# Attention and a gated MLP on one core: every h by half-size products, running sums kept in PSUM, and new instruction orders

## The chip, the cores and the metric

The kernel runs on one core of a Trainium2 chip. The metric is the device time of one execution in microseconds, as the median of several runs. Of the core's engines, TensorE (PE) multiplies matrices into PSUM (eight banks of 512 float32 per partition), ScalarE (ACT) and VectorE (DVE) work element by element on PSUM and SBUF, GpSimd (POOL) on SBUF, and SyncE (SP) issues most transfers. Each engine works off its own queue in order; semaphores tie the queues together.

## What is computed

Batch 8, 8 heads, 576 positions, head size 64. A linear attention with cosine and sine weights gives x, 4608 tokens of 512; an MLP with 2048 hidden units follows.

```
r(x) = max(x, 0);  q_p = [r(q) cos, r(q) sin],  k_p = [r(k) cos, r(k) sin]     (per position)
kv  = k_p^T v,   z = sum(k_p)
x   = (q_p kv) / (q_p z + 1e-6)              -> (4608, 512)
h   = x @ w_in                               -> (4608, 2048)
g   = h * sigmoid(beta * h)
out = g @ w_out                              -> (4608, 512)
```

## The kernel before

**Tiling.** The 4608 tokens are cut into nine chunks of 512 (0 to 8), the hidden units into 16 tiles of 128 (`jt`). Chunk c of the MLP runs beside the attention of batch c+1, so that PE has work of both kinds. Matmuls are bfloat16 into float32 PSUM. All PSUM is one tile `ps` of eight banks, and the code names banks by number.

**A chunk** has an h part (`xt`, the transposed x of the chunk, times `win`, then a silu on ACT into `g_t`), the attention of its batch (K: k times v into two banks, copied to `kv`; N: the numerators in three parts of two banks each, `num_all`; x: denominator, reciprocal and product on DVE, `x_part` at L319, then a transposing DMA into the next chunks' `xt`), and an output part (`g_t` times `wout`). Around them run the preparation of the next batch's inputs: k relus (ACT, L192), v times sine (ACT, `v`, L218) and cosine (DVE, `w`, L220), q relus (DVE, `q`), the q turn by a transposing DMA (L259), q times the tangent on GpSimd (`g`, L223), and loads of raw q, k and v by SP.

**Half-size products.** Where a 2 by 2 block product would take eight block products, seven are enough, with sums of blocks of the weights (`wh_sums`, `w_sums`, DVE, once), of x (`x_sum`, four per chunk, `t1` to `t4`) and of g (`g_sum`, S1 to S4, L404). For a pair of h tiles each block is 128 rows of weights twice by 256 tokens, so that a pair takes 14 matmuls of 256 columns (L473) in place of eight of 512 (L427). The output goes so in chunks 1 to 8 (`o_fast`, L552, 56 matmuls for each half of the tokens), h in part: four pairs of chunks 3 to 6 (X, Y, Z, V) and six of chunks 7 and 8; the other tiles are plain (`h_plain`, p0 to p7). Chunk 2 takes all h plain (`h_first`).

**A pair's seven products** in `h_fast` use three banks. Bank b gathers 1, 6, 7 and 4, bank e gathers 5 and 3, bank a holds 2. Between them c1 copies b to SBUF (ACT, L498), c5 copies e (DVE, L499), cu copies b again after 6 (ACT, L500), a2 adds c1 to a (DVE, L501), a7 adds c5 to b into b's second half (L502), a3 adds cu to e into a's second half (L503). Then Sa and Sb take the silu of banks a and b (L418). `o_fast` does the same with all three copies on ACT (L598 to L600), adds into the output tile `o_sb` (L602 to L604) and a last copy c4 (L572).

**Order.** The order within chunks 3 to 8 is written out by hand in three strings, `ORDER` (chunks 3 to 6), `ORDER_END` (7) and `ORDER_LAST` (8); `chunk` (its dispatch) records the instructions in this order, engine by engine, and `manual_schedule` keeps it. Loads of the next raw tiles go out when the last reader of the present one is recorded. The q turn (N) waits for the last silu, GpSimd's q product for the first c5 (`after`). `SPLITS` cuts some matmuls of chunks 2 to 5 in two. Stores are issued by GpSimd up to chunk 6, then by SP, and in chunk 8 by SP and ACT.

Of the kernel before, what the change touches and what calls it, by code (L numbers as in the profile page):

```python
# [22 lines left out]
def kernel(  # L23
# [349 lines left out]
    def h_bank(c, jt):  # L373
        if c < 2 and jt < 4:
            return ((3, 2, 5, 0), (6, 7, 4, 5))[c][jt]
        return ((6, 7, 4, 5) if c == 0 else (0, 1, 4, 5))[jt % 4]
# [38 lines left out]
    def h_silu(c, jt, bank):  # L415
        if (c, jt // 4) not in gs:
            gs[c, jt // 4] = gt_pool.tile([P, 4, TCH], BF16, name="g_t", tag="g_t")
        return nc.scalar.activation(gs[c, jt // 4][:, jt % 4], ps[:, bank], AF.Silu, scale=beta[:, jt : jt + 1])  # L418

    def h_plain(c, jt, bank, cols=1):  # L420
        xt = xt_tile(c)
        w = NB // cols
        for mi in range(MI):
            jp, g = divmod(mi, 2)
            for o in range(0, NB, w) if mi else (0,):
                z = o + w if mi else NB
                nc.tensor.matmul(ps[:, bank, o * 64 : z * 64], lhsT=win[jt // 4][:, mi, (jt % 4) * P : (jt % 4 + 1) * P],  # L427
                                 rhs=xt[:, o:z, jp, g * HP : (g + 1) * HP],
                                 start=(mi == 0), stop=(mi == MI - 1 and z == NB))

    def wx_tiles():
# [6 lines left out]
            BF16)[:, 0 : 4 * NB // 2 * P].rearrange("q (s n c) -> q s n c", s=4, n=NB // 2)  # L438
# [6 lines left out]
    def wh_sums(jt):  # L445
        f0 = jt % 4
        A11, A12, A21, A22 = (win[jt // 4][:, 2 * jp : 2 * jp + 2, f * P : (f + 1) * P]
                              for f in (f0, f0 + 1) for jp in range(2))
        s1, s2, s3, s4 = (w_sum(jt, i) for i in range(4))
        nc.vector.tensor_tensor(s1, A21, A22, op=ALU.add)  # L450
        nc.vector.tensor_tensor(s3, A11, A21, op=ALU.subtract)
        nc.vector.tensor_tensor(s2, s1, A11, op=ALU.subtract)
        return nc.vector.tensor_tensor(s4, A12, s2, op=ALU.subtract)

    def x_sums(c):
        xt, n = xt_tile(c), NB // 2
        X11, X12, X21, X22 = (xt[:, i * n : (i + 1) * n, jp] for jp in range(2) for i in range(2))
        t1, t2, t3, t4 = (wx["x"][:, i] for i in range(4))
        nc.vector.tensor_tensor(t1, X12, X11, op=ALU.subtract)
        nc.vector.tensor_tensor(t2, X22, t1, op=ALU.subtract)  # L460
        nc.vector.tensor_tensor(t3, X22, X12, op=ALU.subtract)
        nc.vector.tensor_tensor(t4, X21, t2, op=ALU.subtract)

    def h_fast(c, jt0, banks):

        b_bank, e_bank, a_bank = banks
        hf = TCH // 2
        b_ps, e_ps, a_ps = (ps[:, k, 0:hf] for k in banks)
        xt, n = xt_tile(c), NB // 2

        def prod(dst, left, right, start, stop):
            for g in range(2):
                nc.tensor.matmul(dst, lhsT=left[:, g], rhs=right[:, :, g * HP : (g + 1) * HP], start=start and g == 0,  # L473
                                 stop=stop and g == 1, skip_group_check=True)
# [5 lines left out]
        def x(jp, i):  # L480
            return xt[:, i * n : (i + 1) * n, jp]

        s1, s2, s3, s4 = (w_sum(jt0, i) for i in range(4))
        t1, t2, t3, t4 = (wx["x"][:, i] for i in range(4))
        p1 = part.tile([P, HM], FP32, name="p1", tag="p1")
        p5 = part.tile([P, HM], FP32, name="p5", tag="p5")
        u = part.tile([P, HM], FP32, name="u", tag="u")

        acc = dict(op=ALU.add)
        ops = {  # L490
            "1": lambda: prod(b_ps, w(0, 0), x(0, 0), True, False),
            "5": lambda: prod(e_ps, s1, t1, True, False),
            "6": lambda: prod(b_ps, s2, t2, False, False),
            "2": lambda: prod(a_ps, w(0, 1), x(1, 0), True, True),
            "7": lambda: prod(b_ps, s3, t3, False, False),
            "3": lambda: prod(e_ps, s4, x(1, 1), False, True),
            "4": lambda: prod(b_ps, w(1, 1), t4, False, True),
            "c1": lambda: nc.scalar.copy(p1, b_ps),  # L498
            "c5": lambda: nc.vector.tensor_copy(p5, e_ps),  # L499
            "cu": lambda: nc.scalar.copy(u, b_ps),  # L500
            "a2": lambda: nc.vector.tensor_tensor(a_ps, a_ps, p1, **acc),  # L501
            "a7": lambda: nc.vector.tensor_tensor(ps[:, b_bank, hf:TCH], b_ps, p5, **acc),  # L502
            "a3": lambda: nc.vector.tensor_tensor(ps[:, a_bank, hf:TCH], e_ps, u, **acc),  # L503
            "Sa": lambda: h_silu(c, jt0, a_bank),
            "Sb": lambda: h_silu(c, jt0 + 1, b_bank),
        }
# [27 lines left out]
    SPLITS = {2: (0, 11), 3: (5, 0), 4: (0, 8), 5: (3, 0)}  # L534
    made = {}

    def late(c):
        made[c] = made.get(c, 0) + 1
        return made[c] > 14 - SPLITS.get(c, (0, 0))[1]

    def o_fast(c, pr, banks):
# [3 lines left out]
        last = c == NTC - 1 and pr == 1  # L545

        def prod(dst, left, right, start, stop, pieces=False):
            order = (0, 1, 2, 3, 4, 5, 7, 6) if c + 1 >= B else range(JT // 2)
            for i in order:
                w = HM // 2 if i and pieces else HM  # L550
                for m in range(0, HM, w):
                    nc.tensor.matmul(dst[:, m : m + w], lhsT=left(i), rhs=right[:, i, m : m + w],  # L552
                                     start=start and i == 0,
                                     stop=stop and i == order[-1], skip_group_check=True)
# [16 lines left out]
        def c4():  # L571
            nc.scalar.copy(o2[:, 0:HM], b_ps)  # L572
            if last:
                store(c, pr + 2, o2, 0, HM)

        def stored(key, op):
            def do():
                op()
                waits[key[0]].discard(key[1:])
                if not last and not waits[key[0]]:  # L580
                    store(c, pr + (2 if key[0] == "2" else 0), o2 if key[0] == "2" else o1)
                elif last and key == "1a2":
                    store(c, pr, o1, 0, HM, nc.sync)
                elif last and key[1] == "a":
                    store(c, pr + (2 if key[0] == "2" else 0), o2 if key[0] == "2" else o1, HM, DM)
# [5 lines left out]
            "1": lambda: prod(b_ps, g_part(0, 0), B11, True, False, late(c)),  # L591
            "5": lambda: prod(e_ps, s_part(S1), T1, True, False, late(c)),
            "6": lambda: prod(b_ps, s_part(S2), T2, False, False, late(c)),
            "2": lambda: prod(a_ps, g_part(1, 0), B21, True, True, late(c)),
            "7": lambda: prod(b_ps, s_part(S3), T3, False, False, late(c)),
            "3": lambda: prod(e_ps, s_part(S4), B22, False, True, late(c)),
            "4": lambda: prod(b_ps, g_part(1, 1), T4, False, True, late(c)),
# [8 lines left out]


# [265 lines left out]
    def k_piece(b, j):  # L873
        if b >= B:
            return
        k_relu(b, j, j + 1, "act")
        if j == 3 and b + 1 < B:
            load_raw(b + 1, "k")

    ORDER = (  # L880
        "p0 Y1 X1 c1X p1 X5 c5X g0 g1 sp0 X6 X2 K c1Y X3 cuX kt Y6 X7 p2 a2X a3X Y5 sp1 a7X cuY c5Y Y7 Z1 SaX "
        "X4 c1Z p3 Y3 Y2 SbX sp2 a7Y Z2 s01 Y4 Z5 sp3 Z6 s03 a3Y a2Z p4 SbY V1 a2Y c5Z cuZ Z7 s02 a7Z p5 "
        "SaY c1V V6 Z3 s11 sp4 s12 cuV a3Z V2 Z4 s14 sp5 V5 SbZ c5V V7 p6 a2V V3 SaZ a7V a3V s21 sp6 SaV "
        "p7 s04 s13 V4 s22 SbV s23 sp7 s24 s31 s33 N0 k1 s32 ox1 c1o ox5 k3 c5o k2 ox6 s34 x0 k0 "
        "ox3 oy1 cuo c1y x2 o3x ox2 ox7 v8 oy5 x1 c5y o2x oy6 w8 q0 q1 cuy v2 v6 oy3 o7x v3 w1 oy7 w4 w3 "
        "w7 o7y ox4 v5 t3 w5 oy2 v4 c4x o3y v7 t1 w0 oy4 w6 t2 v1 c4y v0 o2y w2 t4")
    ORDER_LAST = (
        "E1 c1E E2 F1 X1 a2E c1X c1F X5 X2 E5 X6 c5X E6 cuX c5E cuE X3 a2X Y1 E3 X7 a3X c1Y a3E SaX a7X "
        "E7 SaE F6 Y5 F5 a7E X4 Y2 c5F Y6 SbX F2 F3 a2Y c5Y a2F cuF E4 Z1 Y3 cuY SbE c1Z a3F Y7 F7 a3Y "
        "SaF a7Y a7F SaY V1 Z6 Z5 V5 c5V Y4 V2 c1V SbY cuZ F4 Z2 V3 c5Z V6 Z3 p4 Z7 a2V cuV SbF sp4 a3V "  # L890
        "p5 SaV a2Z sp5 a3Z SaZ p6 s13 s01 a7Z Z4 V7 p7 a7V V4 sp6 s11 s03 SbZ ox1 s21 s22 SbV sp7 oy1 "
        "s12 s14 s31 ox2 c1o s32 s02 s34 oy2 s04 oy5 s33 c1y o2x s23 ox6 cuo o2y s24 ox5 ox7 c5y c5o o7x "
        "ox3 oy6 cuy o3x ox4 c4x oy7 o7y oy3 oy4 o3y c4y")
    ORDER_END = (
# [127 lines left out]
    for c in range(2, NTC):  # L1022
# [29 lines left out]
        if c == FAST - 1:  # L1052
            x_sums(c + 1)
# [45 lines left out]
```

## Time and profile before

| what | value |
|---|---|
| median of 3 runs | 277.19 us (276.81 to 278.05) |
| span of the profiled execution | 275.5 us |
| granted clock of PE, mean | 0.999 |
| DMA | 54.0 MB, mean 196 GB/s |
| silu on ACT, 128x512 (L418) | 0.697 us each, 96 of them |
| add on DVE into PSUM, 128x256 (L501 to L503) | 0.42 to 0.43 us |
| copy on ACT, 128x256 (L498, L500) | 0.375, 0.384 us |
| x product on DVE, 128x768 (L319) | 0.957 us |
| q product on GpSimd (L223) | 2.38 us |

The profile is of one execution; its span reaches from the first instruction to the last. Times of single instructions overlap within an engine: the next one starts before the last has written out, so that the spacing of two is shorter than the length of one. A line number names the code line that recorded an instruction.

### The profile page before, as it was taken

The numbers are of one execution on the slowest core, as the hardware profiler recorded it, in microseconds if no ns is written. First come the engines' busy times: TensorE is split into PE (matmuls) and PEld (weight loads), VectorE is DVE, ScalarE is ACT, GpSimd is POOL, SyncE is SP. The second block draws the span as 40 slices with busy tenths as digits, with TensorE's granted clock in tenths as the row PEclk, the third lists the DMA queues.
The fourth block names the chain that finished last, engine by engine and source line by source line (L and its number), as shares of the span: only waits on it lengthen the run. The fifth ranks groups of instructions, "written<-read, shape, count | busy, mean of one in ns | idle before, by whom it ended". The sixth has DMA issues, their size and how long they took to land.

```text
span 275.5 us, 9048 instructions
## 1 busy us (share of the span) xinstructions
PE 268.3 (97%) x3749; PEld 199.8 (73%) x3749; DVE 220.7 (80%) x580; ACT 186.2 (68%) x381; POOL 67.5 (24%) x87
## 2 busy tenths in 40 slices
PE   8899999999999999999999999999999999999993
PEld 8554455456875599869866998688668886888683
DVE  5989969599999899599959985899589589558851
ACT  5778677788238657796669756986694289429821
POOL 1444000500087003800390038102810140000000
PEclk9999999999999999999999999999999999999999
DMA  7999999999969999938893798075400740032005
GB/s 241 370 396 384 392 389 303 385 201 379 240 151 299 209 347 261 366 118 122 195 382 148 119 238 293 28 107 107 114 2 12 117 115 2 1 87 68 2 23 130
DMA packets 50745, 54.00 MB, mean 196 GB/s; under 512 B 31232, under 2 KB 31760, under 8 KB 50704
## 3 DMA queue, kind: packets, MB, share of 16 engines
q1 hardware_dynamic: 47744, 45.88, 59.9%
q0 software_dynamic: 2688, 7.34, 8.7%
q8 instruction: 29, 0.48, 0.7%
q10 hardware_dynamic: 272, 0.21, 0.3%
q14 instruction: 12, 0.10, 0.1%
HBM read 36.71 MB, written 9.44 MB: 168 GB/s over the span
## 4 chain that ended last, share of the span: by engine, by line
PE 86%; DMA 9%; DVE 2%; SPq 1%; issue 1%; ACTq 0%; ACT 0%; DVEq 0%
PE ps L552 36%; PE ps L473 16%; PE ps L427 13%; PE ps L384 12%; DMA raw_q<-in_q_dram 6%; PE ps L297 4%; DMA raw_v<-in_v_dram 3%; PE ps L522 3%; PE ps L276 2%; SPq L79 1%; DVE xs L319 1%; PE ps L235 0%; PE ps L356 0%; DVE win L115 0%; DVE vb L210 0%
## 5 line engine op out<-in xcount | busy, mean ns | idle before, releaser
L418 ACT ACTIVATE g_t<-ps,beta 128x512 bf16<-128x512 f32 x96 | 60.9, 697 | 3.2 <-DVE ps L503 2.8
L515 POOL DMA_DIRECT2D out_dram<-o_sb x56 | 33.1, 597 | 118.1 <-DVE o_sb L602 43.4
L552 PEld LDWEIGHTS <-S 128*128 128x128 bf16 x589 | 51.4, 98 | 5.1
L384 PE MATMUL ps<-xt,win 128*128 128x512 bf16 (+1 forms) x196 | 42.8, 375 | 0.1
L552 PEld LDWEIGHTS <-g_t 128*128 128x128 bf16 x440 | 38.2, 98 | 4.1
L427 PE MATMUL ps<-xt,win 128*128 128x512 bf16 (+1 forms) x184 | 40.8, 351 | 0.0
L392 ACT ACTIVATE g_t<-ps,beta 128x512 bf16<-128x512 f32 x48 | 32.3, 689 | 7.2 <-PE ps L384 7.1
L384 PEld LDWEIGHTS <-win 128*128 128x128 bf16 x196 | 18.8, 98 | 21.0 <-issue 0.2
L552 PE MATMUL ps<-wout,g_t 128*128 128x256 bf16 (+1 forms) x284 | 31.7, 262 | 0.0
L552 PE MATMUL ps<-wout,S 128*128 128x256 bf16 (+1 forms) x305 | 31.5, 255 | 0.0
L552 PE MATMUL ps<-T,S 128*128 128x256 bf16 (+1 forms) x284 | 30.8, 262 | 0.0
L404 DVE TENSOR_TENSOR S<-g_t 128x512 bf16<-128x512 bf16 (+1 forms) x66 | 26.1, 423 | 3.6 <-ACT g_t L418 2.7
L218 ACT ACTIVATE vb<-raw_v,sin 128x256 bf16<-128x256 f32 (+1 forms) x58 | 25.9, 501 | 2.2 <-DMA raw_v<-in_v_dram 2.2
L473 PEld LDWEIGHTS <-w_stage 128*128 128x128 bf16 x224 | 21.6, 98 | 6.7
L473 PE MATMUL ps<-w_stage 128*128 128x256 bf16 x168 | 26.2, 272 | 0.0
L427 PEld LDWEIGHTS <-win 128*128 128x128 bf16 x184 | 17.9, 98 | 10.1
L319 DVE TENSOR_TENSOR xs<-ps,rden 128x768 bf16<-128x768 f32 (+4 forms) x26 | 22.8, 884 | 0.8
L220 DVE TENSOR_SCALAR vb<-raw_v,cos 128x256 bf16<-128x256 f32 x63 | 20.0, 374 | 0.8 <-DMA raw_v<-in_v_dram 0.8
L473 PEld LDWEIGHTS <-win 128*128 128x128 bf16 x168 | 16.4, 98 | 4.7 <-issue 0.3
L223 POOL TENSOR_TENSOR qs<-qt,tanr 128x1152 bf16<-128x1152 bf16 x6 | 14.2, 2381 | 21.4 <-DVE den L308 21.0
L473 PE MATMUL ps<-xt,win 128*128 128x256 bf16 x112 | 19.1, 272 | 0.0
L599 ACT COPY p<-ps 128x256 f32<-128x256 f32 x16 | 5.9, 372 | 16.9 <-PE ps L552 13.8
(105 smaller groups left out, 418.3 us busy)
## 6 DMA issues: line engine op xcount, KB each, us to landing
raw_v<-in_v_dram SPq DMA_DIRECT2D x7, 1152.0 KB, 10.8
raw_k<-in_k_dram SPq DMA_DIRECT2D x7, 1152.0 KB, 7.5
raw_q<-in_q_dram SPq DMA_DIRECT2D x7, 1152.0 KB, 7.4
out_dram<-o_sb POOLq DMA_DIRECT2D x56, 128.0 KB, 4.1
w_stage<-in_moe_w_in_dram SPq DMA_DIRECT2D x3, 1024.0 KB, 13.9
w_stage<-in_moe_w_out_dram SPq DMA_DIRECT2D x2, 1024.0 KB, 8.8
w_stage<-in_moe_w_out_dram SPq DMA_DIRECT2D x4, 512.0 KB, 11.9
out_dram<-o_sb SPq DMA_DIRECT2D x12, 128.0 KB, 2.4
```

The lines of the kernel that those rows point to most:

```text
L218: nc.scalar.activation(o, a, AF.Copy, scale=t[:, n : n + 1])
L220: nc.vector.tensor_scalar(o, a, scalar1=t[:, n : n + 1], scalar2=None, op0=ALU.mult)
L223: return eng.tensor_tensor(dst.rearrange("q n (g p) -> q n g p", g=2), src.rearrange("q n (g p) -> q n g p", g=2), tanr[:, n0:n1].unsqueez ...
L319: nc.vector.tensor_tensor(o.rearrange("q j n s d -> q j (n s) d"), nv[:, :, a:z, :, 0:D].rearrange("q j n s d -> q j (n s) d"), rden[:, :, ...
L384: nc.tensor.matmul(ps[:, h_bank(c, jt), i * 64 : (i + w) * 64], lhsT=win[jt // 4][:, mi, (jt % 4) * P : (jt % 4 + 1) * P], rhs=xt[:, i : i ...
L392: return nc.scalar.activation(gs[c, jt // 4][:, jt % 4], ps[:, h_bank(c, jt)], AF.Silu, scale=beta[:, jt : jt + 1])
L404: return nc.vector.tensor_tensor(o, l, r, op=op)
L418: return nc.scalar.activation(gs[c, jt // 4][:, jt % 4], ps[:, bank], AF.Silu, scale=beta[:, jt : jt + 1])
L427: nc.tensor.matmul(ps[:, bank, o * 64 : z * 64], lhsT=win[jt // 4][:, mi, (jt % 4) * P : (jt % 4 + 1) * P], rhs=xt[:, o:z, jp, g * HP : (g ...
L473: nc.tensor.matmul(dst, lhsT=left[:, g], rhs=right[:, :, g * HP : (g + 1) * HP], start=start and g == 0, stop=stop and g == 1, skip_group_ ...
L515: (eng or own).dma_start(out=out_v[bb, n][:, m0:m1], in_=o_sb[hf * HP : (hf + 1) * HP, m0:m1])
L552: nc.tensor.matmul(dst[:, m : m + w], lhsT=left(i), rhs=right[:, i, m : m + w], start=start and i == 0, stop=stop and i == order[-1], skip ...
```

## The change

All eight pairs of h go by half-size products in chunks 3 to 8, by `h_pair`; the output of chunks 2 to 8 by `o_pair`. Chunk 1 keeps `o_fast`; chunk 2 keeps its plain h, with two tiles in other banks. Both new functions share `fast_ops`, which uses two banks for a pair. Bank b's halves hold the running sum (1, 6, 7, 4) and product 5. c (the seed) copies the running sum into the first half of bank a, where product 2 adds; d or D copies product 5 to SBUF on ACT or DVE; e adds that copy to the running sum after 6, into the second half of bank a, where 3 adds; f does the same after 7, into the second half of b (for the output, into `o_sb`). A and B take the silu of a whole bank (for the output, A or X copies bank a, 512 wide, on ACT or DVE, B or Y the first half of b).

The order is now one string for each of chunks 2 to 8, and names the bank of every product 1, seed, K and N. Tokens: `h35` is product 5 of pair 3, `h3c7` its seed into bank 7, `oxe` the e of the output's first token half, `s13` S1 of tiles 6 and 7, `W71` sum 1 of the weights of pair 7, `TQ` the q turn of the next batch, `Lv` a load; x, k, v, w, q, g and t as above. The t sums of two chunks lie in two places (`4 * (c % 2)`), so that they can be made while the last ones are read. The weight sums of pairs 1, 3, 5 and 7 are made in chunk 3. The q turn and GpSimd's q products wait for their data alone, the kv copy is on ACT (`kT`), and `SPLITS` is gone.

```diff
@@ h_bank, h_silu, wx_tiles
+        if c == 2 and jt in (10, 11):
+            return jt - 8
-        return nc.scalar.activation(gs[c, jt // 4][:, jt % 4], ps[:, bank], AF.Silu, scale=beta[:, jt : jt + 1])
+        return nc.scalar.activation(gs[c, jt // 4][:, jt % 4], bank, AF.Silu, scale=beta[:, jt : jt + 1])
-            BF16)[:, 0 : 4 * NB // 2 * P].rearrange("q (s n c) -> q s n c", s=4, n=NB // 2)
+            BF16).rearrange("q (s n c) -> q s n c", s=8, n=NB // 2)
...
+    def sum_tile():
+        tag = ("p5", "p1", "u")[len(sums) % 3]
+        sums.append(part.tile([P, HM], FP32, name=tag, tag=tag))
+        return sums[-1]
+
+    def fast_ops(left, right, prod, finish):
+        st = {}
+        def bank(key):
+            return ps[:, st[key]]
+        def at(key, hf):
+            return bank(key)[:, hf * HM : (hf + 1) * HM]
+        def first(n):
+            st["b"] = n
+            prod(at("b", 0), left(0), right(0), True)
+        def seed(n):
+            st["a"] = n
+            nc.scalar.copy(at("a", 0), at("b", 0))
+        def keep(eng):
+            st["p5"] = sum_tile()
+            (nc.scalar.copy if eng == "act" else nc.vector.tensor_copy)(st["p5"], at("b", 1))
+        def add(dst):
+            nc.vector.tensor_tensor(dst, at("b", 0), st["p5"], op=ALU.add)
+        return {
+            "1": first,
+            "5": lambda: prod(at("b", 1), left(1), right(1), False),
+            "c": seed,
+            "d": lambda: keep("act"),
+            "D": lambda: keep("dve"),
+            "6": lambda: prod(at("b", 0), left(2), right(2), False),
+            "2": lambda: prod(at("a", 0), left(3), right(3), False),
+            "e": lambda: add(at("a", 1)),
+            "7": lambda: prod(at("b", 0), left(4), right(4), False),
+            "3": lambda: prod(at("a", 1), left(5), right(5), False),
+            "f": lambda: finish(add),
+            "4": lambda: prod(at("b", 0), left(6), right(6), False),
+        }, bank, at
+
+    def h_pair(c, i):
...
+        ops, bank, at = fast_ops(lefts.__getitem__, rights.__getitem__, prod, lambda add: add(at("b", 1)))
+        ops["A"] = lambda: h_silu(c, jt0, bank("a"))
+        ops["B"] = lambda: h_silu(c, jt0 + 1, bank("b"))
...
+    def o_pair(c, pr):
...
+        def finish(add):
+            add(sb_tile("2")[:, HM:DM])
+            stored(1)
+        def take(key, eng):
+            copy = nc.scalar.copy if eng == "act" else nc.vector.tensor_copy
+            if key == "a":
+                copy(sb_tile("1"), bank("a"))
+                store(c, pr, sb["1"])
+            else:
+                copy(sb["2"][:, 0:HM], at("b", 0))
+                stored(0)
...
+        4: (
+            "g1 h114 h15 h015 h05 h211 K02 h1d h0d h0c7 K1 h1c0 h06 h0e h16 h25 kT h12 h312 h02 h2D h03 h2c6 h07 h1e "
+            "h17 h13 h0A h3c7 h0f h26 h1f h413 h1A h04 g0 h2e h45 h4c0 h0B h35 h4D h36 h23 h14 h27 h3d h22 h2f h46 h1B "
+            "h3e h515 h55 h24 h2A h2B h37 h32 h33 h5D h714 h4e h75 h616 h3f h43 h5c1 h34 h3A h6c7 h47 h56 h7d s10 h42 "
+            "h66 h3B h4f h65 h44 h7c2 h6d h62 s20 h5e h76 h52 h57 h4B h53 h6e h7e h5f h63 h73 h72 h4A h77 h5A h67 s11 "
+            "TQ N00 w5 h7A w7 h6f h7f h54 h6A s21 oy13 h74 h64 v6 ox12 v8 x0 N10 h5B s30 s12 h6B s33 h7B oyc7 w1 N25 "
+            "s13 s22 v4 oy5 x1 v5 s23 s42 ox5 oxc4 oxd k2 s32 oy2 oy6 k1 s31 oyd v3 w2 w4 s41 ox6 s40 oye t1 ox2 oy7 "
+            "v7 k3 q0 oxe q1 s43 oyf k0 ox7 w3 t2 v2 w0 oxf oy3 oy4 x2 w8 ox3 oyA v0 w6 oyB v1 Lv Lk oxA ox4 t3 t4 oxY"),
...
-    FAST = 3
+    h_first(2)
     for c in range(2, NTC):
...
+        chunk(c)
```

The last tokens of chunk 8 are `oxY oy3 oy2 oyY oyA`.

## The prediction

> **What bounds the kernel now.** First the page's busy shares and the chain that ended last:
>
> ```profile
> PE 268.3 (97%) x3749; PEld 199.8 (73%) x3749; DVE 220.7 (80%) x580; ACT 186.2 (68%) x381; POOL 67.5 (24%) x87
> PE 86%; DMA 9%; DVE 2%; SPq 1%; issue 1%; ACTq 0%; ACT 0%; DVEq 0%
> ```
>
> TensorE (PE) is busy for 97% of the span and makes up 86% of the chain. The chain's 9% of DMA lies before 40 us, in code that the change leaves alone. Next the chain in order of time, for the unit prices (start, length, what, how many matmuls):
>
> ```profile
> 139.93 1.15 PE ps L276 x72
> ...
> 151.38 1.38 PE ps L297 x130
> ...
> 180.91 12.33 PE ps L552 x112
> ...
> 221.23 6.78 PE ps L473 x62
> 228.01 0.86 PE ps L427 x4
> ```
>
> A 512-column matmul of a plain h costs 0.864/4 = 0.216 us; a 256-column matmul of a half-size product costs 6.78/62 = 0.1093. K (k times v) costs 1.15, the numerators N 1.38. Then busy time chunk by chunk (chunk 2 after its h, chunks 3 to 8, the tail):
>
> ```profile
> core 0: us, PE busy (x) PEld busy (x) DVE busy (x) ACT busy (x) POOL busy (x), PEclk, DMA share, GB/s
> 95.09:109.09 14.00, 14.00 (x334) 13.41 (x335) 12.24 (x35) 8.99 (x21) 2.28 (x5) 1.00 1.13 290
> 109.09:137.11 28.02, 28.02 (x433) 23.26 (x431) 23.41 (x66) 20.63 (x44) 9.17 (x10) 1.00 0.75 204
> 137.11:165.24 28.13, 28.13 (x474) 22.59 (x472) 23.41 (x65) 21.03 (x45) 9.30 (x11) 1.00 0.81 225
> 165.24:193.25 28.01, 28.01 (x426) 22.69 (x425) 23.76 (x70) 21.05 (x45) 8.92 (x10) 1.00 0.55 132
> 193.25:221.23 27.98, 27.98 (x418) 21.84 (x417) 20.76 (x56) 15.68 (x33) 8.95 (x11) 1.00 0.31 60
> 221.23:246.15 24.92, 24.92 (x214) 20.73 (x213) 18.10 (x51) 15.95 (x36) 2.06 (x4) 1.00 0.19 46
> 246.15:270.40 24.25, 24.25 (x206) 19.96 (x205) 16.58 (x45) 15.91 (x36) 0.00 (x0) 1.00 0.22 50
> 270.40:275.50 5.10, 0.86 (x8) 0.52 (x6) 0.42 (x1) 0.37 (x1) 0.00 (x0) 0.97 0.48 118
> ```
>
> The reader is to see that PE has no gap from chunk 2 on, at full clock. So what PE no longer does is gained, as long as ScalarE (ACT) and VectorE (DVE) keep up. Their pace comes from the timeline of chunk 4:
>
> ```profile
> 143.72 2.43 ACT L418 ACTIVATE g_t<-ps,beta 128x512 bf16<-128x512 f32 x4
> ...
> 147.06 0.36 ACT L498 COPY p<-ps 128x256 f32<-128x256 f32 x1
> 147.32 0.70 ACT L418 ACTIVATE g_t<-ps,beta 128x512 bf16<-128x512 f32 x1
> ...
> 147.43 0.42 DVE L404 TENSOR_TENSOR S<-g_t 128x512 bf16<-128x512 bf16 x1
> 147.88 0.42 DVE L404 TENSOR_TENSOR S<-S,g_t 128x512 bf16<-128x512 bf16 x1
> ```
>
> Four silus (0.69 each) take 2.43, so one follows another after (2.43-0.69)/3 = 0.58; a copy holds ACT for 0.26 to 0.27. Where an instruction needs its own engine's previous result (S2 needs S1) it starts at 0.45 instead of at 0.33, the spacing of independent ones: 0.03 after the end.
>
> **What PE loses.** A pair of h by half-size products takes 14 x 0.1093 = 1.53, plain 8 x 0.216 = 1.73. After the change a chunk 3 to 6 is 112 x 0.1093 = 12.24 of h, 12.24 of output, K and N: 27.01. Four of them are 108.04 against 112.14: -4.10. Chunk 7 falls to 24.48 from 24.92: -0.44. Chunk 8 really ends at 270.40+0.86, so it falls from 25.11 to 24.48: -0.63. Chunk 2's output loses the matmuls cut into 128 columns (SPLITS): 12.24 + 1.36 of N against 14.00: -0.40. Sum with no stall: -5.57. It includes the 0.1 us or so of gaps and split costs that each chunk has now.
>
> **What ACT and DVE get.** Per pair, three copies and three adds become a seed (ACT, PSUM to PSUM), one copy and two adds. But all eight pairs have them now. ACT work per pair is two silus 1.16 + seed 0.27 + 5/8 of a copy 0.17 = 1.60, against 1.53 of PE. So in the h part ACT becomes as slow as PE, where today half of the pairs are plain and ask for silus alone. Seeds have a second price: in the changed program's waits, five of a steady chunk's eight seeds write a bank that the silu just ahead of them on ACT is still reading, so they wait for ACT's own end: 0.69+0.03 instead of 0.58, some 0.14 each. No row shows this wait on ACT; from below it is 0, from above 0.14 by the DVE row, which I take.
>
> Chunk 4 walked to the place where it binds: the first silu needs the 12th product of PE's order, with K ahead of it, 12 x 0.2186 + 1.15 = 3.77, and ACT starts 0.21 later (silus in chunk 2 start 0.21 after the last matmul's turn ends): 3.98. Before pair 7's seed ACT has 8 silus 4.64, six copies 1.62 and five such waits 0.70: the seed starts at 10.94, is done at 11.31 (0.37), and PE may go on 0.05 later (a copy of kv ended at 11.97, the matmul behind it began at 12.02): 11.36. PE wants it for product 6 of pair 7 after 44 products, at 44 x 0.2186 + 1.15 = 10.77. Stall 0.59; with no own-wait cost, none. Behind it on PE stands the rest of the chunk. Orders 5 and 6 are the same up to bank numbers. For the three I take 0.55 each: 1.65.
>
> Chunk 3 has four seeds of this kind and sixteen weight sums more on DVE (W; eight of them came in chunk 5 so far, eight are new) at 0.20 spacing: 3.2. DVE's queue in chunk 3 is then 25.6 (W 3.2, S 5.3, adds and copies of h 6.3, x 4.0, output 1.7, w 2.35, q 1.36, t 1.33; by their spacing in the timeline: 0.33 for an S, an add or a t, 0.26 a w, 0.68 a q, 1.33 an x with its reciprocal) of 27.0. Behind a late W stands product 5 of a pair, behind a late S the output's product 5. I take 0.8, between 0 and 1.6. Chunks 7 and 8 have no K and no v, but also less PE work between their silus: 0.4 each. Given back in all: 1.65+0.8+0.8 = 3.25, with bounds 0.5 and 6.5.
>
> **Edits at no cost.** The kv copy moves from DVE to ACT (0.59), in the 1.15 of K in which ACT has little to do; uncovered, it delays the first silu by as much. The q turn (a transposing DMA on SP's queue, which today waits behind the silus) goes out at a chunk's start, past nothing on SP but the loads, and lands before N some 13 us later. GpSimd's two q products (2.38 each) no longer wait for a copy; N comes late enough to hide both and the stores queued around them. The v load is used earlier: ACT takes v5 at some 13.6 us into chunk 3, today its first v at 20. The load went out at 109.32 and such loads took up to 11.9, so it lands at 121.2, 12.1 into the chunk. Cover 1.5; if it is gone, each us is a us of PE, since the last silus stand behind v5 on ACT.
>
> **Tail.** The last product is now followed by a 512-column ACT copy (0.60 by L528) and 128 KB stores (2.4 to landing) in place of a 256-column copy (0.37) and 64 KB (2.0 to 2.2): +0.5, bounds 0.2 and 0.8.
>
> **A rule against the change.** PSUM halves that used to sit in three banks share one now, and the changed program guards by bank: a seed waits for product 5 too (0.22), product 6 for both copies (0.27). Today product 5 has a bank of its own. The Trainium skill, page "PSUM — Partial Sum Buffer", section "PSUM bank collisions raise a hardware error", asks for just that: guard by bank, not by address. By it every pair's chain is 0.22+0.27 longer; by the walk above this is hidden behind other pairs' products, so the sum would differ only if eight banks were too few. The page "ScalarE: Activation LUTs" ("Step-by-step: what each stage is for") speaks the other way: ACT writes PSUM faster than SBUF. No run here shows it yet; it would shorten the 0.37.
>
> **Sum.** -5.57 + 3.25 + 0.5 = -1.8 on the span of 275.5: 273.7. The median of the runs lies 1.7 above that span (277.19): 275.4.
>
> **Rivals.** (1) ACT is not the limit: own-engine waits cost nothing and DVE's load spreads. For it: the walk then has no stall at all. Against: ACT has 1.60 of work per 1.53. -5.57+0.3+0.5: 272.4. (2) Given back nearly whole: stalls of 0.8 to 1 in every chunk, since an output stage whose DVE work (13 S, x, w, q, t and its adds, by the same prices some 15 us, in 13.7 of PE) sits behind late silus adds its own. -5.57+5.3+0.5: 277.4. (3) Slower, by one mechanism: the seed. No row shows ACT writing PSUM; if it takes 0.1 longer than a copy to SBUF (by the rows of the copies 0, by DVE's adds, 0.42 into PSUM against 0.42 into SBUF, 0 too), eight seeds in six ACT-bound chunks add 4.8: 280.2. It decides from 0.067 each: 1.8+1.4 = 3.2 over 48 seeds. That the products are not really replaced is excluded by the program's matmul count.
>
> **How the numbers follow.** 0.5% (1.4 us) is about what a measurement of this kernel can tell from no change: 275.8 and 278.6 are the limits. Forecast, 273.9 to 276.4: 0.46, of which 0.33 below 275.8. Rival 1: 0.25. Rival 2: 0.17. Rival 3: 0.12. Faster 0.33+0.25 = 0.58, same 0.13+0.17 = 0.30, slower 0.12. The range 272.6 to 277.8 leaves out rival 3 and the ends of 1 and 2.
>
> **What would show it.** Right: chunks 4 to 6 some 27.6 long, with PE idle of about 0.5 each just ahead of products 6 of the later pairs, put down to ACT; ACT without a gap between first silu and last; chunk 3 longest; PE's sum 5 us smaller. Wrong: chunks of 27.0 (rival 1), gaps in the output part put down to DVE (rival 2), seeds over 0.45 (rival 3), or ACT waiting for a v load.

## The result, and the profile after it

| | before | after |
|---|---|---|
| median, us (four runs each) | 277.16 (276.81 to 278.05) | 284.25 (283.40 to 284.38) |
| span of the profiled execution, us | 275.5 | 281.6 |
| mean granted clock of PE | 0.999 | 0.988 |

The changed kernel takes 1.0243 times as long (95% interval 1.0223 to 1.0264): slower, and outside the predicted range. First the page of the changed kernel: busy time, PE and its clock in forty slices (tenths), the chain that ended last.

```profile
PE 268.9 (95%) x3712; PEld 208.0 (74%) x3712; DVE 225.6 (80%) x588; ACT 192.7 (68%) x391; POOL 67.0 (24%) x87
PE   8899999999999999399999999999999999999993
PEclk9999999999999999689999999999999999999999
PE 82%; ACT 6%; DMA 3%; issue 3%; DVE 3%; SPq 1%; DVEq 0%
```

The shares differ little from before. The rows by slices say where to look: in the seventeenth PE has a 3, and the clock has 6 and 8 in place of 9 in this one and the next. A slice is 7 us. Now busy time chunk by chunk (chunks 3 to 8, each from the end of the last matmul before it):

```profile
core 0: us, PE busy (x) PEld busy (x) DVE busy (x) ACT busy (x) POOL busy (x), PEclk, DMA share, GB/s
108.58:143.80 35.22, 30.30 (x443) 25.10 (x441) 31.65 (x83) 23.86 (x52) 9.21 (x11) 0.90 0.54 148
143.80:171.76 27.96, 27.68 (x442) 24.08 (x441) 23.43 (x65) 22.98 (x51) 9.64 (x12) 1.00 0.65 192
171.76:199.73 27.97, 27.70 (x443) 24.05 (x441) 22.39 (x64) 22.95 (x50) 8.92 (x11) 1.00 0.72 167
199.73:227.71 27.98, 27.70 (x442) 24.07 (x441) 19.89 (x53) 17.31 (x37) 8.93 (x11) 1.00 0.30 61
227.71:252.31 24.60, 24.60 (x226) 21.86 (x225) 17.69 (x48) 15.03 (x32) 2.48 (x5) 1.00 0.22 59
252.31:277.41 25.10, 24.82 (x225) 21.67 (x222) 15.96 (x43) 15.39 (x34) 0.00 (x0) 1.00 0.24 56
```

Chunk 3 takes 35.22 where it took 28.02 before: +7.20, more than the whole loss. The chunks 4 to 6 are 0.21 shorter together (84.12 to 83.91), chunk 7 is 0.32 shorter, chunk 8 with the tail 0.06. The rest of the span's difference is a start of chunk 2's output that lies 0.39 earlier (94.70 in place of 95.09) and 0.12 less in that output (13.88 in place of 14.00): 7.20-0.21-0.32-0.06-0.39-0.12 = 6.1. So the question is chunk 3 alone. Two windows of it (columns as above), and the instructions around them (start, length, engine, line, tiles, in brackets the idle time before it and what ended it):

```profile
111.84:117.09 5.25, 0.39 (x4) 0.20 (x3) 5.25 (x3) 0.15 (x1) 4.70 (x2) 0.83 1.04 397
117.09:122.14 5.05, 5.04 (x24) 3.49 (x24) 2.86 (x11) 3.08 (x6) 0.00 (x0) 0.50 0.91 174
```

```profile
110.93 0.29 DVE L443 TENSOR_TENSOR w_stage<-win 128x256 bf16<-128x256 bf16 x1
111.13 5.57 DVE L443 TENSOR_TENSOR w_stage<-win,w_stage 128x256 bf16<-128x256 bf16 x1
116.62 0.42 DVE L487 TENSOR_TENSOR ps<-ps,u 128x256 f32<-128x256 f32 x1
...
111.83 4.71 POOL L223 TENSOR_TENSOR w_stage<-qt,tanr 128x1152 bf16<-128x1152 bf16 x2
...
111.63 0.60 PE L511 MATMUL ps<-xt,win 128*128 128x256 bf16 x4
117.09 0.58 PE L511 MATMUL ps<-xt,win 128*128 128x256 bf16 x2 [4.86 <-DVE ps L487]
```

Read from below. PE waits 4.86 for an add on DVE (L487). The add stands in DVE's queue behind one sum of weight blocks (L443), and that sum takes 5.57 where its like take 0.28 to 0.29. It ends at 116.70, when GpSimd's two q products end (111.83+4.71 = 116.54). The idle time has a second price: from 117.09 the granted clock is 0.50 for 5.05, in which 24 matmuls run that take 24 x 0.1093 = 2.62 at full clock, so 2.43 more. 4.86+2.43 = 7.29, which is all of the 7.20.

In the kernel before, the same two products ran at nearly the same time, and the sign was there:

```profile
76.69 4.73 POOL L223 TENSOR_TENSOR qs<-qt,tanr 128x1152 bf16<-128x1152 bf16 x2 [20.98 <-DVE den L308]
79.53 4.14 DVE L220 TENSOR_SCALAR vb<-raw_v,cos 128x256 bf16<-128x256 f32 x9
...
109.89 0.29 DVE L453 TENSOR_TENSOR w_stage<-win,w_stage 128x256 bf16<-128x256 bf16 x1
112.04 4.72 POOL L223 TENSOR_TENSOR w_stage<-qt,tanr 128x1152 bf16<-128x1152 bf16 x2 [0.95 <-DVE p L499]
113.12 0.70 DVE L288 CAST kv<-ps 128x520 bf16<-128x520 f32 x1 [1.17 <-PE ps L276]
116.44 0.94 DVE L404 TENSOR_TENSOR S<-g_t 128x512 bf16<-128x512 bf16 x2 [0.52 <-ACT g_t L418]
```

In chunk 3 the weight sums of that kernel were over before GpSimd began behind a copy of DVE, and until 116.44 DVE had copies and adds that read PSUM: nothing was held. The first S sum at 116.44 took 0.60 in place of 0.42 and ended at 117.04, behind GpSimd's end at 116.76. At 79.53, beside another pair of products, nine v products took 4.14 where nine at their spacing of 0.26 take about 2.4: the first alone took 2.04 in place of 0.35 and ended at 81.57, just after GpSimd at 81.42.

### The profile page after: what moved, and what is told of

The parts are those of the page before. It is cut to its first block, busy times and chain, and to the rows that moved or that the text cites. A ratio compares the mean times of both kernels' runs of the same rounds, so it can differ in the third digit from the quotient of the medians.

```text
span 281.6 us, 8955 instructions
## 1 busy us (share of the span) xinstructions
PE 268.9 (95%) x3712; PEld 208.0 (74%) x3712; DVE 225.6 (80%) x588; ACT 192.7 (68%) x391; POOL 67.0 (24%) x87
## 4 chain that ended last, share of the span: by engine, by line
PE 82%; ACT 6%; DMA 3%; issue 3%; DVE 3%; SPq 1%; DVEq 0%
PE ps L620 31%; PE ps L511 21%; PE ps L386 14%; PE ps L543 5%; ACT g_t L420 4%; PE ps L562 4%; PE ps L297 4%; DMA raw_v<-in_v_dram 3%; PE ps L276 3%; ACT ps L480 1%; DVE ps L487 1%; DVE xs L319 1%; SPq L79 1%; PE ps L356 0%; DVE win L115 0%
## 5 line engine op out<-in xcount | busy, mean ns | idle before, releaser
L511 PE MATMUL ps<-w_stage 128*128 128x256 bf16 x288 | 48.2, 277 | 0.9 <-ACT ps L480 0.7
L511 PEld LDWEIGHTS <-w_stage 128*128 128x128 bf16 x384 | 38.0, 100 | 7.9 <-issue 2.1
L487 DVE TENSOR_TENSOR ps<-ps,p 128x256 f32<-128x256 f32 x74 | 30.5, 428 | 16.4 <-PE ps L511 7.8
L386 PE MATMUL ps<-xt,win 128*128 128x512 bf16 (+1 forms) x196 | 42.8, 375 | 0.1
L511 PE MATMUL ps<-xt,win 128*128 128x256 bf16 x192 | 35.3, 278 | 5.1 <-DVE ps L487 4.9
L480 ACT COPY ps<-ps 128x256 f32<-128x256 f32 x62 | 22.4, 370 | 12.7 <-PE ps L620 8.6
L620 PE MATMUL ps<-wout,g_t 128*128 128x256 bf16 x224 | 28.8, 273 | 0.0
L620 PE MATMUL ps<-T,S 128*128 128x256 bf16 x224 | 27.0, 273 | 0.0
L620 PE MATMUL ps<-wout,S 128*128 128x256 bf16 x224 | 26.7, 273 | 0.0
L487 DVE TENSOR_TENSOR ps<-ps,u 128x256 f32<-128x256 f32 x36 | 15.4, 428 | 6.8 <-PE ps L511 4.8
```

The lines of the kernel that those rows point to most:

```text
L386: nc.tensor.matmul(ps[:, h_bank(c, jt), i * 64 : (i + w) * 64], lhsT=win[jt // 4][:, mi, (jt % 4) * P : (jt % 4 + 1) * P], rhs=xt[:, i : i ...
L480: nc.scalar.copy(at("a", 0), at("b", 0))
L487: nc.vector.tensor_tensor(dst, at("b", 0), st["p5"], op=ALU.add)
L511: nc.tensor.matmul(dst, lhsT=l[:, g], rhs=r[:, :, g * HP : (g + 1) * HP], start=start and g == 0, stop=g == 1, skip_group_check=True)
L620: nc.tensor.matmul(dst, lhsT=l(i), rhs=r[:, i], start=start and i == 0, stop=i == order[-1], skip_group_check=True)
```

## The experiments

**What made chunk 3 long.** Theory A: a DVE instruction that takes two tiles from SBUF is held while a GpSimd product runs. The test takes GpSimd's products of batch 4 out of chunk 3 and puts them behind the last S sum of chunk 2, where DVE has x products, reading PSUM, to do. The rival, B: the q turn, now at a chunk's start, is what delays it.

```diff
         2: (
-            "oy16 N22 x2 N00 oy5 ...
+            "oy16 G0 G1 N22 x2 N00 oy5 ...
         3: (
-            ... h1A h23 W52 g0 "
+            ... h1A h23 W52 "
...
-            ... h72 s11 g1 h7A ...
+            ... h72 s11 h7A ...
+            elif k_ == "G":
+                q_tan(b + 1, n, None if n else last_sum)
...
```

> Edit: GpSimd's two q products of batch 4 (2.38 us each) are recorded at the start of chunk 2's output part, behind chunk 2's last S sum on DVE, instead of in chunk 3; all else as in the changed kernel. Theory A (GpSimd's products and DVE's sums of two SBUF operands shut each other out: the weight sum at 111.13 that took 5.57 us ended 0.2 us after GpSimd's pair of products): no weight sum over 0.3 us in chunk 3, PE's 4.9 us gap gone, no half clock behind it, chunk 3 28 to 29 us instead of 35.4, total 284.3 - 6.5 to 7.5 = 277 to 278. Theory B (the q turn, which now goes out at the start of chunk 3 and took 9.8 us, slows DVE's SBUF accesses): the long sum stays, total 283 to 285. Theory C (the sixteen weight sums of chunk 3 are simply too much for DVE): chunk 3 stays over 31, total over 280.

Measured: 276.6 us (276.1 to 278.48), ratio to before 0.9978 [0.9955, 1.0000], a little under the 277 to 278 of theory A. Three lines of its timeline:

```profile
97.69 4.74 POOL L223 TENSOR_TENSOR w_stage<-qt,tanr 128x1152 bf16<-128x1152 bf16 x2 [10.12 <-DMA qt<-qb]
...
101.29 1.29 DVE L443 TENSOR_TENSOR w_stage<-win 128x256 bf16<-128x256 bf16 x1
...
112.42 0.28 DVE L443 TENSOR_TENSOR w_stage<-win,w_stage 128x256 bf16<-128x256 bf16 x1
```

The weight sum that took 5.57 takes 0.28, and the loss of 7 us is gone with it. Chunk 3 lasts 28.28 from its K to the next one's with all sixteen weight sums in it, so theory C falls. GpSimd issues stores from 108.75 to 113.22, so beside stores alone this sum is not held. In chunk 2 one weight sum still meets the products: started at 101.29, it lasts 1.29, to 102.58, just after GpSimd's end at 102.43. So 7 us hang on which instruction of DVE meets the same work of GpSimd.

The rival's test, the q turn back behind the last silu:

```diff
-                    q_turn_dma(b + 1)
+                    q_turn_dma(b + 1, last)
```

> Edit: the q turn of chunks 3 to 5 waits for the last silu recorded ahead of it, as in the kernel before; GpSimd's products stay where the changed kernel has them. Theory A: the weight sum of some 5.6 us stays at the start of chunk 3, total 283.5 to 285. Theory B: the long sum is gone, total 277 to 279.

Measured: 283.52 (282.89 to 284.13), 1.0212 [1.0173, 1.0251], with the same sum of 5.57 and the same wait of 4.86. B falls.

**Is it the guard, or what DVE does meanwhile?** Two more kernels leave the products in chunk 3 and give them a guard again, one behind weight sum W53, one behind W74, the chunk's last.

```diff
-                wh_sum(2 * n, int(op[2]))
+                parts[op] = wh_sum(2 * n, int(op[2]))
...
-                q_tan(b, n)
+                q_tan(b, n, parts.get("W53"))
```

> The changed kernel, with GpSimd's two products of chunk 3 held back by a guard, as in the kernel before, here behind the weight sum W53. Theory A: they run from about 116.5 to 121.2, and the next DVE instruction with two SBUF inputs, S sum s30 due at 117.5, is held to about 121.2 (some 3.7 us in place of 0.42), the copies and adds behind it with it; PE idles 3 to 3.7 and the time is 279 to 282, the upper end if PE's clock halves again. Rival theory (it was the missing guard as such, or the products' early start, that cost the time): with the guard back, 276 to 277.

> The changed kernel, with GpSimd's two products of chunk 3 behind the chunk's last weight sum W74. Theory A: they run from about 118.1 to 122.9, where DVE has only copies and adds on PSUM until the S sums due at 121.4; these are held 1.4, and N (due at 122.4) waits some 0.5 for the products: 276.0 to 277.5, no sum over 2 us. Rival (any GpSimd product in chunk 3 costs what it cost): over 280.

Measured: 280.69 (278.68 to 281.48), 1.0092 [1.0062, 1.0121], behind W53, and 278.18 (277.34 to 279.44), 1.0027 [1.0007, 1.0047], behind W74, a little over its range. The timeline behind W53:

```profile
116.22 4.90 POOL L223 TENSOR_TENSOR w_stage<-qt,tanr 128x1152 bf16<-128x1152 bf16 x2 [3.95 <-DVE w_stage L443]
...
117.13 0.43 DVE L487 TENSOR_TENSOR ps<-ps,p 128x256 f32<-128x256 f32 x1
117.47 1.41 DVE L406 TENSOR_TENSOR S<-g_t 128x512 bf16<-128x512 bf16 x1
118.81 2.46 DVE L443 TENSOR_TENSOR w_stage<-win,w_stage 128x256 bf16<-128x256 bf16 x1
...
122.10 0.38 PE L511 MATMUL ps<-w_stage 128*128 128x256 bf16 x2 [1.95 <-ACT ps L480]
```

The add on PSUM at 117.13 keeps its 0.43 beside GpSimd; the S sum behind it takes 1.41 and the weight sum 2.46, to GpSimd's end. The S sum got through where GpSimd's first product gives way to its second (116.22+2.4); so the hold was by the product here. The forecast of one sum held for the whole time was wrong in that, and its 3 to 3.7 of idle PE too long (about 2.4, 2.1 of it in one piece); the time lies in its range. Behind W74 two S sums took 2.13 in place of 0.75, and PE waited 0.28 for the products and 0.80 for an add. A guard helps as far as it moves the products beside DVE work that is not held.

The clock has a part in these runs too. In the profiled one, at full clock, PE idles those 2.4 (by the spacing of its matmuls); of ten runs six had a mean clock of 0.990 to 0.994 and took 281.05 on average, four had 0.997 to 1.000 and took 278.92. The drop came with some of the runs only, and these took 2.1 longer; whether PE also idled longer in them isn't shown.

**What the chunks 4 to 6 give back.** With chunk 3 mended, PE's gaps are few: 0.20 and 0.40 ahead of the seeds of pairs 6 and 7 in each of the chunks 4 to 6, 0.40 in chunk 8, none in chunk 7, some 0.6 in chunk 3. That is the forecast stall. (These gaps go by the spacing of the starts; the brackets of the timeline count from the modelled end of the matmul before, and have 0.23 for 0.40.) ACT shows why (chunk 4 of the changed kernel):

```profile
147.71 0.69 ACT L420 ACTIVATE g_t<-ps,beta 128x512 bf16<-128x512 f32 x1
148.43 0.36 ACT L480 COPY ps<-ps 128x256 f32<-128x256 f32 x1
148.70 0.69 ACT L420 ACTIVATE g_t<-ps,beta 128x512 bf16<-128x512 f32 x1
...
155.10 0.38 PE L511 MATMUL ps<-w_stage 128*128 128x256 bf16 x2 [0.23 <-ACT ps L480]
```

A seed behind a silu of its own bank starts 0.72 after that silu's start, not 0.58. To test it, the seeds of pairs 5 to 7 go to DVE (a new token C), once on the changed kernel and once with the early products.

```diff
+        def seed_dve(n):
+            st["a"] = n
+            nc.vector.tensor_copy(at("a", 0), at("b", 0))
...
-            ... h43 h5c1 h34 h3A h6c7 h47 h56 h7d s10 h42 "
-            "h66 h3B h4f h65 h44 h7c2 h6d h62 s20 h5e ...
+            ... h43 h5C1 h34 h3A h6C7 h47 h56 h7d h42 "
+            "h66 h3B h4f h65 h44 h7C2 h6d s10 h62 s20 h5e ...
```

> Edit: in chunks 4 to 6 the seeds of pairs 5, 6 and 7 are copied by DVE instead of ACT, and S1 of tiles 0 and 1 is taken a few places later; chunk 3 as in the changed kernel. Theory D (in chunks 4 to 6 PE waits for ACT, whose seeds start 0.72 us behind the silu that they must wait for, not 0.58): ACT is relieved by 3 x (0.27 + 0.14) = 1.2 us ahead of pair 7's product 6, the 0.84 us that the h part loses per chunk falls to 0.3 or less, chunks 4 to 6 go from 27.97 to 27.2 to 27.5, total 284.3 - 1.5 to 2.3 = 282 to 282.8. Rival E (the loss comes from PSUM banks that come free late, or from DVE): no change within 0.4, or slower, since DVE gets 3 x 0.33 us more.

> Edit: the products early and the DVE seeds together. Theories A and D: the gains add, 284.3 - 7 - 2 = 275 to 276, which is 0.4 to 0.8% below the kernel before. If either falls: 277 or more.

Measured: 284.72 (283.81 to 285.87), 1.0265 [1.0224, 1.0306], and with the early products 277.7 (276.76 to 279.02), 1.0007 [0.9983, 1.0030]: no gain. In the second:

```profile
147.98 0.42 DVE L406 TENSOR_TENSOR S<-g_t 128x512 bf16<-128x512 bf16 x1
148.43 0.43 DVE L406 TENSOR_TENSOR S<-S,g_t 128x512 bf16<-128x512 bf16 x1
148.78 0.42 DVE L491 TENSOR_TENSOR ps<-ps,u 128x256 f32<-128x256 f32 x1
...
149.25 0.38 PE L516 MATMUL ps<-xt,win 128*128 128x256 bf16 x2 [0.62 <-DVE ps L491]
```

ACT's stall is gone, and PE waits 0.62 for an add that now stands behind two S sums. Next, the two sums behind the adds of pair 5; and, on top, the weight sum that was held in chunk 2 moved behind the q relus, and the seed of pair 4 of chunk 8 on DVE.

```diff
-            "h66 h3B h4f h65 h44 h7C2 h6d s10 h62 s20 h5e h76 h52 h57 h4B h53 h6e h7e h5f h63 ...
+            "h66 h3B h4f h65 h44 h7C2 h6d h62 h5e h76 h52 h57 h4B h53 h6e h7e h5f s10 s20 h63 ...
```

> As the run with GpSimd's products in chunk 2 and the seeds of pairs 5 to 7 on DVE, but the two S sums of chunks 4 to 6 that stood before the adds e of pair 5 now stand behind f of pair 5. Theory D (ACT's own-engine waits cost 0.60 of PE a chunk, and with the seeds on DVE the two sums, 0.8 on DVE, cost the 0.78 gap in their place): the gap before product 3 of pair 5 goes and no other comes, chunks 4 to 6 are 27.3 to 27.4 long in place of 27.96, and the time is 276.6 - 1.8 = 274.8. Rival (what is short is the chain of copies and adds itself, wherever the sums stand): a gap of 0.4 to 0.8 stays in each of the chunks 4 to 6, time 276.5 to 277.7.

> As the run before it, with the first sum of the weights of pair 6 moved behind the two q relus in chunk 2 (it was held 1.0 us by GpSimd's products) and with the seed of pair 4 in chunk 8 on DVE (PE waited 0.40 for it on ACT). Theory A (DVE sums of two SBUF tiles are held while GpSimd's product runs, DVE work on PSUM or with one SBUF tile is not): no DVE sum over 0.45 us in chunk 2, PE's gap of 0.55 there is gone, though GpSimd works in the same 4.7 us; with chunk 8 another 0.4: 0.9 less than the run before it, 273.9. Rival (GpSimd slows any DVE work beside it): the gap in chunk 2 stays, 274.4.

Measured: 276.22 (275.41 to 278.38), 0.9956 [0.9933, 0.9978], and 276.25 (276.01 to 278.54), 0.9959 [0.9936, 0.9982]. Misses by 1.4 and 2.3. The gaps of the h part are gone, but chunk 4 lasts 28.09 from its K to the next one's: PE now stalls in the output part, ahead of N for an x product on DVE and once more behind it (0.35 and 0.32). In chunk 8 DVE's seed made two gaps, 0.48 and 0.43, out of one of 0.40. The chunk 2 part held: GpSimd worked from 97.04 to 101.77, no sum of DVE lasted over 0.45, PE had no gap. The sentence on single SBUF tiles, though, has the v products at 79.53 against it, and no run here tests them.

The two moves alone (products and weight sum), all seeds on ACT:

> The changed kernel with GpSimd's products of batch 4 in chunk 2 and the weight sum that they held there moved behind the q relus; all seeds on ACT. Theory A: PE's gap of 0.55 in chunk 2 goes, the 0.60 in each of the chunks 4 to 6 and the 0.40 in chunk 8 stay: 276.6 - 0.5 = 276.1. Rival (the gap in chunk 2 is covered by a later wait anyway): 276.6.

Measured: 276.41 (276.03 to 277.62), 0.9958 [0.9940, 0.9976]; the gap of 0.55 is gone from its trace, but the time, between the two forecasts, can't tell them apart. With earlier seeds on DVE, those of pairs 3 and 4 (`h3c7` to `h3C7`, `h4c0` to `h4C0`, and `h5c6` to `h5C6` in chunk 8):

> As the run with the two moves, and the seeds of pairs 3 and 4 of chunks 4 to 6, and of pair 5 in chunk 8, on DVE: there DVE waits (0.73 and 0.77 in chunk 4, 0.95 in chunk 8) while ACT has no gap. Theory E (ACT and DVE share one sum of work, and work moved costs only where the taker has no idle time before its own queue is full, in chunk 4 from 149 on): PE's gaps of 0.60 go without new ones in the output part, chunks 4 to 6 are 27.4 in place of 27.96, chunk 8 0.4 shorter: 2.1 less than the run with the two moves, 274.0. Rival (whatever ACT is relieved of, DVE gives back later, as with the seeds of pairs 5 to 7): chunks 4 to 6 stay at 27.8 to 28.0, time 275.6 to 276.2.

Measured: 277.54 (277.02 to 279.0), 1.0000 [0.9981, 1.0019]. A miss, and worse than none:

```profile
141.81 0.43 DVE L484 COPY ps<-ps 128x256 f32<-128x256 f32 x1 [0.83 <-ACT g_t L420]
142.15 0.75 DVE L491 TENSOR_TENSOR ps<-ps,p 128x256 f32<-128x256 f32 x2
...
142.62 0.38 PE L516 MATMUL ps<-w_stage,win 128*128 128x256 bf16 x2 [0.48 <-DVE ps L491]
```

The seed waits on DVE until a silu of ACT has ended (0.83), and two adds that were ready stand behind it; PE waits for one of them. A seed whose bank a silu on ACT still reads is tied to ACT on either engine. What is not tied is the copy of product 5, whose product is done early. So, with all seeds on ACT, first the copy of pair 7 goes to DVE, then also that of pair 3:

```diff
-            ... h56 h7d s10 h42 "
+            ... h56 h7D s10 h42 "
...
-            ... h14 h27 h3d h22 h2f ...
+            ... h14 h27 h3D h22 h2f ...
```

> As the run with the two moves, and in chunks 4 to 6 the copy of product 5 of pair 7 on DVE in place of ACT, where DVE waits 0.77 with nothing to do and the copy's product is long done, so that nothing on DVE waits behind it. Theory E (work moved off ACT pays if the taker has idle time and does not have to wait for the mover): PE's gap ahead of seed 7 falls by the 0.27 that a copy holds ACT, the earlier 0.20 stays: 0.33 a chunk in place of 0.60, in all 0.8 less than with the two moves: 275.6. Rival (DVE always gives it back): no shorter.

> As the run before, with the copy of product 5 of pair 3 on DVE as well (there DVE has 0.1 free at once and 0.77 within 2.3 us). Theory E: PE's gaps ahead of seeds 6 and 7 fall by another 0.27 to under 0.1, chunks 4 to 6 are 27.4 to 27.5 long: 1.6 less than with the two moves, 274.8. Rival: a new gap behind an add or copy on DVE takes it back, chunks 27.9, 276.4.

Measured: 276.0 (275.37 to 277.88), 0.9955 [0.9937, 0.9974], and 275.93 (274.99 to 276.39), 0.9942 [0.9922, 0.9962]. The one copy takes the gap of 0.40 down to 0.12, as expected; its time fell by 0.4, not 0.8, which is within the spread of the runs. With both copies, first from the list of waits (in total, times, longest), then the windows of the chunks 4 to 6:

```profile
PE ps L511 <- ACT ps L480: 0.2, 1, 0.2
```

```profile
136.77:164.29 27.52, 27.52 (x442) 24.16 (x441) 24.21 (x67) 22.40 (x49) 9.68 (x12) 1.00 0.66 195
164.29:191.72 27.43, 27.43 (x442) 24.08 (x441) 22.98 (x66) 22.38 (x48) 8.91 (x11) 1.00 0.77 170
191.72:219.15 27.43, 27.43 (x442) 24.08 (x441) 20.53 (x55) 16.75 (x35) 8.91 (x11) 1.00 0.29 62
```

The only wait of PE for a seed that is left is that of chunk 8, and the chunks 4 to 6 take 27.52, 27.43 and 27.43, without a gap over 0.1. This version has the lowest median of all, below the kernel before by 0.4 to 0.8%. Its time fell short of the expected 274.8 by 1.1, though the trace has the gaps closed as expected: its profiled run was one of the two fastest (274.99, span 273.0), so the difference seems to lie in what varies between runs, which I did not follow.

## Why the prediction was wrong

**The step that failed** is among the edits at no cost: "GpSimd's two q products (2.38 each) no longer wait for a copy; N comes late enough to hide both and the stores queued around them." It asked who needs the products and when, and that was right: N never waited for them in the changed kernel. It did not ask who works beside them. The products ran beside the weight sums that the change had added to chunk 3; one was held for 5.57, PE idled 4.86 behind it, and the half clock after that cost 2.43: 7.29 in a place that stood at nothing in the sum. Taking the products away from that place, and nothing else, brought 284.25 to 276.6, with 275.4 predicted. The wait for a copy, in the kernel before, put the products where DVE read PSUM.

The Trainium skill has this rule: the page "SBUF — State Buffer", section "Who interferes with whom", says that a DVE instruction with two SBUF inputs contends with a GpSimd instruction that reads SBUF, that whichever is issued first holds the shared ports for its whole instruction and that the other blocks fully. The runs agree for the sums (5.57 and 1.29 beside products, 0.28 without) and for the adds on PSUM (0.43 beside a product). One thing differs, if the recorded start is the moment of issue: the sum of 5.57 was recorded as started at 111.13, 0.70 ahead of the products' own start, and lasted through both products, while behind W53 a sum got through between two. Why one passed and the other not stays open.

The other terms, in turn:

- *Work that PE loses.* Too large. In the version without gaps, a chunk of 27.43 consists of 12.51 for h, 1.15 for K, 1.44 for N and 12.33 of output, where the floor of 27.01 had 12.24, 1.15, 1.38 and 12.24: the changes between kinds of matmul, about 0.1 each, were left out. Three chunks lost 1.74 (84.12 to 82.38), not 3.09, and chunk 2's output lost 0.12 in place of 0.40. For the chunks 7 and 8 it came to 24.60 and 25.10 less a gap of 0.40, against 24.48.
- *Given back to ACT, chunks 4 to 6.* Right in cause, place and size: 0.59 walked, 0.55 taken, 0.60 measured, ahead of the seeds of the last two pairs, put down to ACT. The own-engine wait was 0.72 against 0.58, as estimated from a DVE row. Chunk 8: 0.40 for 0.40. Chunk 7: none for 0.40. Chunk 3 without the held sum: some 0.6 for 0.8.
- *The seed* took 0.370 in the mean of 62 copies from PSUM to PSUM, as much as a copy to SBUF (0.377). That excludes the rival that was slower by the seed, and gives nothing of the shorter time that the Trainium skill's page "ScalarE: Activation LUTs", section "Step-by-step: what each stage is for", promises for PSUM.
- *Tail.* +0.5 forecast, none measured: 5.10 less the 0.86 of PE work in its window is 4.24 before, 4.19 after.
- *The rivals.* The one that ended slower named the seed; the loss came by a mechanism that none of the three had. The first fell with the own-engine wait of 0.72 and the stall of 0.60. The second, output stage on DVE, was not what slowed this kernel; that DVE has little room there showed only when seeds had gone to DVE (0.35 and 0.32 in chunk 4).

Without any held sum the kernel took 276.41, 1.0 above the forecast of 275.4 and inside its range: PE's loss was too large by 1.35 in the chunks 4 to 6 alone, and chunk 7 and the tail gave 0.9 of it back. So the nearness is partly luck: errors of opposite sign.

## What to carry to other kernels

When an edit lets an engine start earlier, ask two questions: who waits for its result, and which instructions of the other engines will run beside it from now on. For work on GpSimd go through DVE's queue over that stretch and look for instructions with two SBUF inputs, and for others that read SBUF, like the v products; put it beside work on PSUM, and keep a guard that holds it there even where the data would allow an earlier start. When an engine is short, move what has been ready for long and has no wait (here a copy, 0.27 a piece), since a moved instruction that waits for the engine it came from holds up everything behind it on the new one.

## What the runs showed of the hardware

- One held DVE sum costs more than its own wait. After 4.86 without a matmul PE ran at a granted clock of 0.50 for 5.05. Behind W53, where PE idled about 2.4 in the profiled run and kept its clock, six runs of ten had a lower mean clock. The skill's page "TensorE: Matmul & The Clock Gate", section "HAM oscillation — how this bites in real kernels", puts the limit at idle gaps of some 3.4 us. The first number agrees with it; the second was not expected from it, and those six runs have no trace, so how long PE idled in them isn't known.
- The held sum counts as busy time of DVE in the profile, not as idle time with a releaser: the window of 5.25 has DVE busy for all of it. Only the length of a single instruction against its like gives it away.
- A held DVE instruction ended the same short time after the product that held it: 0.15 or 0.16 for 128x256 (weight sums that ended at 116.70, 102.58 and 121.27, the v product at 81.57), 0.28 for an S sum of 128x512 (the one started at 116.44 in the kernel before, at 117.47 behind W53).
- GpSimd's products took 2.37 to 2.41 each in all runs, held DVE work beside them or not, but for one: the second behind W53, at whose start the S sum got through, took 2.56.
